# Turning u for the channel MLP: 96 TensorE transposes replaced by transposing DMAs of 16-bit halves

## The chip, the cores and the metric

The kernel runs on one core of a Trainium2 chip. The metric is the device time of one launch in microseconds (us); lower is better. The kernel before takes 856.54 us, the median of three runs from 856.44 to 856.61.

A core has five engines that run side by side, each with its own instruction stream in program order: TensorE (PE in the profile; PEld is its weight load), VectorE (DVE), ScalarE (ACT), GpSimd (POOL) and SyncE (SP). SyncE computes nothing here; it issues transfers, which 16 DMA engines carry out. Engines wait for one another on semaphores. An instruction that waits holds back all that stands behind it on its own engine.

## What is computed

A routed attention, then an MLP mixer. There are 4 batches of 768 positions with 8 heads of 64, so the attention gives `x` of 4 x 768 x 512 f32. The change lies in the second part:

```python
xt = x.transpose(0, 2, 1)
h = np.maximum(xt @ w_tok1, 0.0) @ w_tok2      # token MLP, over the 768 positions
u = x + h.transpose(0, 2, 1)
h2 = np.maximum(u @ w_ch1, 0.0) @ w_ch2        # channel MLP, 512 -> 1536 -> 512
return (u + h2).astype(np.float32)
```

TensorE contracts over the partition, the first of the two dimensions of on-chip memory. `u` is kept with positions on the partitions, and `u @ w_ch1` contracts over the 512 features, so `u` has to be turned: features on the partitions, positions along the row. How that turn is made is what the change is about.

## The kernel before, in words

**Stages.** The attention fills the first part of the time. From some 320 us on the token MLP runs, as a list of 32 steps named `ends`: `tok1(b, t)` and `tok2(b, j)`, the latter adding into `xs[b][:, j]`, so that the tile `xs[b]` (128 partitions x 6 x 512 f32) turns from `x` into `u` in place. Beside these steps weights are rounded and summed (`beside`). From 404 us on the channel MLP runs, batch by batch.

**The channel MLP.** Its two layers are each a 2x2 block product with seven products in place of eight, which needs sums of blocks of the weights (`left_weights`, `right_weights`) and of the turned `u` (`R` with T1 to T4). A batch has two parts of the 1536 hidden features. In each part come three first-layer chunks (`ch1_chunk`: hidden features from the turned `u`) and then three second-layer chunks (`ch2_chunk`: back to 512 features, added into `xs[b]`). `chunk` writes out the order of a chunk's products on TensorE: A11·B11, then the *deferred* last product of the chunk before (A22·T4, kept in `late`), then S1·T1, A12·B21, S2·T2, S4·B22, S3·T3. After each product `done` has VectorE or ScalarE empty the PSUM tile. In the first layer ScalarE has six instructions a chunk (L679, L683, L690, L703); in the second layer the chunks have none on ScalarE.

**The turned u.** The tile `uT` holds one batch: 2 halves of the positions (`n`) x 4 groups of 128 features (`f`) x 384 positions. There is one buffer, so a batch's `uT` can be filled only when the last first-layer chunk of the batch before has read it. `turn_u(b, n)` (L590) fills half `n`: for each `f` three TensorE transposes (L599) into a PSUM tile `pt`, then one copy to `uT` (L603), in turn on ScalarE and VectorE. With `n == 1` four subtractions on VectorE follow (T1 to T4, 128x768 f32 each). For batch 0 both calls stand between token steps (L896), when 11 and 9 steps are left. For batch b+1 they stand after the first and second of the three second-layer chunks of batch b's part 1 (L913).

**Outputs.** In part 1 each row `xs[b][:, j]` is stored by SyncE as soon as it is done (L735), 256 KB each.

**A way of turning that is there already.** The attention turns its results with the DMA engines: `values` copies PSUM into `avrows`, low and high 16-bit halves of each f32 apart (L454), `pair_turn` issues a transposing DMA from SyncE, which moves 16-bit elements (L459), and `pair_put` interleaves the halves again into `x` (L472).

The scheduling is manual: each engine's instructions stand in the order in which the program calls them.

Of the kernel before, what the change touches and what calls it, by code (L numbers as in the profile page):

```python
# [8 lines left out]
F32 = mybir.dt.float32  # L9
BF16 = mybir.dt.bfloat16  # L10
U32 = mybir.dt.uint32
U16 = mybir.dt.uint16
# [5 lines left out]
B, H, S, D = 4, 8, 768, 64  # L18
C = 16
P = 128  # L20
NJ = S // P
DM = H * D
NF = DM // P
# [4 lines left out]
HJ = NJ // 2  # L28
HS = HJ * P
# [19 lines left out]
def kernel(  # L49
# [29 lines left out]
    nc = tc.nc  # L79
# [30 lines left out]
    pools = {}  # L110


    ident = const.tile([P, P], F32, name="ident")
# [15 lines left out]
    xs = [xpool.tile([P, NJ, DM], F32, name=f"x{b}") for b in range(B)]  # L129
# [392 lines left out]
    def tok1(b, t):  # L522
        if t == 0:
            h1s[b] = tokpool.tile([P, NT, DM], F32, name="h1", bufs=2)
        pf = mtile([P, DM], "ph1")
        for j in range(NJ):
            nc.tensor.matmul(  # L527
                pf, lhsT=W["tok1"][:, j, t * P : (t + 1) * P], rhs=xs[b][:, j],
                start=(j == 0), stop=(j == NJ - 1),
            )  # L530
        relu(h1s[b][:, t], pf)
# [17 lines left out]
    def sub(dst, a, b):  # L549
        nc.vector.tensor_tensor(out=dst, in0=a, in1=b, op=ALU.subtract)  # L550

    def add(dst, a, b):
        nc.vector.tensor_tensor(out=dst, in0=a, in1=b, op=ALU.add)  # L553

    def left_weights():

        w = W["ch1"]
        half = DCH // 2
        A = {
            f"A{i + 1}{j + 1}": w[:, 2 * j : 2 * j + 2, half * i : half * i + half]  # L560
            for i in range(2)
            for j in range(2)
        }
        extra = pools["wsums"].tile([P, 3, 2, half], F32, name="w1s")
        A["S1"], A["S2"], A["S4"] = (extra[:, i] for i in range(3))
        yield lambda: add(A["S1"], A["A21"], A["A22"])
        yield lambda: sub(A["S2"], A["S1"], A["A11"])
        yield lambda: sub(A["A21"], A["A11"], A["A21"])
        yield lambda: sub(A["S4"], A["A12"], A["S2"])
        A["S3"] = A["A21"]  # L570
        pools["A"] = A
# [15 lines left out]
        B_["T3"] = B_["B12"]  # L587
        pools["B"] = B_

    def turn_u(b, n):  # L590

        if n == 0:
            pools["uT"] = pools["u"].tile([P, 2, NF, HS], F32, name="uT")
            pools["uTs"] = pools["u"].tile([P, 3, NF // 2, HS], F32, name="uTs")
        uT, uTs = pools["uT"], pools["uTs"]
        for f in range(NF):
            pt = pools["ps_m"].tile([P, HJ, P], F32, tag="YZ"[f % 2], name="pt")
            for i in range(HJ):
                nc.tensor.transpose(  # L599
                    out=pt[:, i], in_=xs[b][:, HJ * n + i, f * P : (f + 1) * P], identity=ident  # L600
                )
            copy = nc.vector.tensor_copy if f % 2 else nc.scalar.copy
            copy(out=uT[:, n, f], in_=pt.rearrange("p i t -> p (i t)"))  # L603
        if n == 1:
            R = {"B11": uT[:, 0, 0:2], "B21": uT[:, 0, 2:4], "B22": uT[:, 1, 2:4]}
            R["T1"], R["T2"], R["T4"] = (uTs[:, i] for i in range(3))
            R["T3"] = b12 = uT[:, 1, 0:2]
            sub(R["T1"], b12, R["B11"])
            sub(R["T2"], R["B22"], R["T1"])
            sub(R["T3"], R["B22"], b12)  # L610
            sub(R["T4"], R["B21"], R["T2"])
            pools["R"] = R

    late = []

    def chunk(n, product, done, last=False):

# [40 lines left out]
    def ch1_chunk(part, i):  # L658

        c = 3 * part + i  # L660
        if i == 0:
            pools["h2"] = {
                k: pools["mlp"].tile([P, 3, HS], F32, name="h" + k)
                for k in ("A11", "A12", "A22", "S1", "S2", "S3", "S4")
            }
        A, R, h2 = pools["A"], pools["R"], pools["h2"]
        kept = {}

        def product(psum, a, r, start):
            for k in range(2):  # L670
                nc.tensor.matmul(  # L671
                    psum, lhsT=A[a][:, k, c * P : (c + 1) * P], rhs=R[r][:, k],
                    start=start and k == 0, stop=k == 1, skip_group_check=not start,
                )

        def done(name, psum):
            if name in ("p1", "p5", "u2"):
                kept[name] = pools["mlp"].tile([P, HS], F32, name=name, bufs=2)
                nc.scalar.copy(out=kept[name], in_=psum)  # L679
            elif name == "c11":  # L680
                a = h2["A11"][:, i]
                add(a, psum, kept["p1"])
                nc.scalar.activation(out=a, in_=a, func=ACT.Relu)  # L683
            elif name == "c12":
                kept["c12"] = pools["mlp"].tile([P, HS], F32, name="c12", bufs=2)
                add(kept["c12"], psum, kept["u2"])
            elif name == "c22":
                a = h2["A22"][:, i]
                add(a, psum, kept["p5"])
                nc.scalar.activation(out=a, in_=a, func=ACT.Relu)  # L690

                nc.vector.scalar_tensor_tensor(
                    out=h2["S3"][:, i], in0=kept["c12"], scalar=0.0, in1=h2["A11"][:, i],
                    op0=ALU.max, op1=ALU.subtract,
                )
                nc.vector.scalar_tensor_tensor(
                    out=h2["S1"][:, i], in0=kept["c12"], scalar=0.0, in1=a,
                    op0=ALU.max, op1=ALU.add,
                )
                sub(h2["S2"][:, i], h2["S1"][:, i], h2["A11"][:, i])  # L700
            else:
                a = h2["A12"][:, i]
                nc.scalar.activation(out=a, in_=psum, func=ACT.Relu)  # L703
                sub(h2["S4"][:, i], a, h2["S2"][:, i])

        chunk(HS, product, done)

    def ch2_chunk(b, part, i):

        h2, Bw = pools["h2"], pools["B"]  # L710
        u = {
            f"c{r + 1}{c + 1}": xs[b][:, HJ * r + i, 256 * c : 256 * c + 256]
            for r in range(2)
            for c in range(2)
        }
        kept = {}
        takes = {"p1": "c11", "p5": "c22", "u2": "c12"}
        gives = {"c11": "p1", "c22": "p5", "c12": "u2"}

        def product(psum, a, w, start):  # L720
            for k in range(3):
                nc.tensor.matmul(  # L722
                    psum, lhsT=h2[a][:, k, i * P : (i + 1) * P], rhs=Bw[w][:, 3 * part + k],
                    start=start and k == 0, stop=k == 2, skip_group_check=not start,
                )

        def done(name, psum):
            if name in takes:
                kept[name] = pools["mlp"].tile([P, DM // 2], F32, name=name, bufs=2)
                add(kept[name], psum, u[takes[name]])  # L730
            else:
                add(u[name], psum, kept[gives[name]] if name in gives else u[name])
                if part == 1 and name in ("c12", "c21"):
                    j = i + HJ * (name == "c21")
                    nc.sync.dma_start(  # L735
                        out[b].rearrange("(p j) m -> p j m", p=P)[:, j], xs[b][:, j]
                    )

        chunk(DM // 2, product, done, b == B - 1 and part == 1 and i == 2)

    good = const.tile([P, 3], F32, name="good")
# [79 lines left out]
    ends = [lambda t=t: tok1(0, t) for t in range(NT)]  # L821
# [66 lines left out]
    pools["wsums"] = pool("wsums", 1, side="right")  # L888
    pools["u"] = pool("upool", 1, side="right")
    beside = weights + list(left_weights())  # L890
    while ends:
        for _ in range(-(-len(beside) // len(ends))):
            beside.pop(0)()
        ends.pop(0)()
        if len(ends) in (11, 9):
            turn_u(0, len(ends) == 9)  # L896
    staging.close()
    tokens.close()
    pools["mlp"] = pool("mlp", 1)
# [1 line left out]
    for b in range(B):  # L901
        for part in range(2):
            for i in range(3):
                ch1_chunk(part, i)
                for _ in range(2):
                    if beside:
                        beside.pop(0)()
            for i in range(3):
                if b == B - 1 and part == 1 and i == 2:
                    both = fits_load()  # L910
                ch2_chunk(b, part, i)
                if part == 1 and i < 2 and b + 1 < B:
                    turn_u(b + 1, i)  # L913
            if b == 0:
                (fits_count if part else fits)()
    late.pop()()


    def general():
# [209 lines left out]
```

## Time and profile before

| | |
|---|---|
| time, median of three | 856.54 us |
| span of the profiled execution | 854.8 us |
| mean granted TensorE clock | 0.998 |
| TensorE busy from 404 to 514 us | 110.00 us |
| VectorE, ScalarE busy in the same stretch | 53.07, 19.10 us |
| share of the DMA engines in the same stretch | 0.03 |
| TensorE transposes `pt` at L599 | 96 |
| `uT` copies on ScalarE, on VectorE | 16 of 479 ns, 16 of 558 ns |
| subtractions T1 to T4 | 16 of some 950 ns |
| transposing DMAs of the attention | 16 `avcols`, 15 `ohT` |
| output stores | 24, landing 2.0 us after issue (median) |

How to read the views: a row of the costliest groups gives line, engine, operation, output<-input and count, then busy time and mean duration of one, then the idle time of the engine just before and what ended most of it. A row of a tile gives minimum, median and maximum duration in ns and the times of the first and last start. A row of the timeline gives start, length, engine, line, and in brackets the idle time before it with what ended it. The chain of waits follows the work that ended last back to the start, step by step, to whatever released each step. A TensorE record is longer than the pitch of such records, because matmuls overlap; the chain's pieces are pitches.

### The profile page before, as it was taken

What the parts mean: (1) busy time and instruction counts of PE and PEld (TensorE: products, weight loads), DVE (VectorE), ACT (ScalarE), POOL (GpSimd) and SP (SyncE); (2) the same over time, 40 slices, a digit from 0 to 9 for tenths busy, and PEclk for the clock granted to TensorE, in tenths of its full rate; (3) what the DMA queues carried; (4) which work ended last, traced back from release to release, by engine and by line L of the source; (5) the groups of instructions that cost most, each with busy time, mean ns of one, the idle gap of its engine ahead of it and who ended that gap; (6) DMA issues with size and microseconds to landing.
All of it is one profiled execution on the core that took longest, in us unless ns stands there. A gap on an engine that the chain in (4) does not pass through costs nothing.

```text
span 854.8 us, 10898 instructions
## 1 busy us (share of the span) xinstructions
PE 844.1 (99%) x4198; PEld 516.4 (60%) x4198; DVE 509.8 (60%) x864; ACT 327.9 (38%) x522; POOL 45.6 (5%) x40
## 2 busy tenths in 40 slices
PE   9999999999999999999999999999999999999996
PEld 4444444444444444444587686776866858768675
DVE  6879888989889853985643453424444334443332
ACT  5677678787777663410201202102112031120210
POOL 1001010110101001410000000000000000000000
PEclk9999999999999999999999999999999999999999
DMA  8786576778774323400000010000100000100001
GB/s 150 154 160 131 112 152 138 151 145 146 143 142 96 56 54 107 151 22 0 0 1 1 1 49 25 1 0 1 38 37 1 1 0 25 50 0 1 1 25 54
DMA packets 158365, 53.92 MB, mean 63 GB/s; under 512 B 147168, under 2 KB 151264, under 8 KB 158304
## 3 DMA queue, kind: packets, MB, share of 16 engines
q1 hardware_dynamic: 156704, 52.74, 28.7%
q8 instruction: 35, 0.57, 0.3%
q10 hardware_dynamic: 1600, 0.39, 0.2%
q14 instruction: 26, 0.21, 0.1%
HBM read 34.64 MB, written 6.29 MB: 48 GB/s over the span
## 4 chain that ended last, share of the span: by engine, by line
PE 88%; DVE 8%; issue 1%; SPq 1%; DMA 1%; ACT 0%; DVEq 0%; POOL 0%; POOLq 0%
PE sc L422 16%; PE pX L722 15%; PE pX L671 15%; PE av L447 11%; PE pZ L722 7%; PE pZ L671 7%; PE ph L527 4%; PE pY L722 4%; PE pY L671 4%; PE pu L536 3%; DVE sum L437 2%; PE pt L599 1%; DVE wh L215 1%; DVE wT L220 1%; PE small L483 1%; DVE wh L210 1%
## 5 line engine op out<-in xcount | busy, mean ns | idle before, releaser
L429 ACT ACTIVATE ex<-sc 128x768 f32<-128x768 f32 x192 | 149.2, 812 | 27.7 <-PE sc L422 16.1
L422 PE MATMUL sc<-qkT 64*128 64x384 f32 x768 | 155.1, 482 | 0.0
L437 DVE TENSOR_TENSOR sum<-sum,ex 128x768 f32<-128x768 f32 x128 | 127.7, 997 | 27.4 <-ACT ex L429 15.2
L447 PE MATMUL av<-ex,va 128*64 128x384 f32 x768 | 127.4, 488 | 0.0
L447 PEld LDWEIGHTS av<-ex,va 128*64 128x64 f32 x768 | 53.7, 137 | 71.7 <-issue 67.9
L422 PEld LDWEIGHTS sc<-qkT 64*128 64x128 f32 x768 | 68.5, 187 | 36.3 <-issue 35.7
L679 ACT COPY p<-pX 128x384 f32<-128x384 f32 x24 | 11.4, 475 | 149.7 <-PE pX L671 149.7
L671 PE MATMUL pX<-uT,wc 128*128 128x384 f32 x192 | 67.4, 487 | 0.0
L422 PE MATMUL sc<-ohT 64*128 64x384 bf16 x384 | 63.3, 324 | 0.5 <-DVE ohT L394 0.2
L671 PEld LDWEIGHTS pX<-uT,wc 128*128 128x128 f32 x192 | 36.2, 190 | 24.7 <-issue 1.0
L454 ACT COPY avrows<-av 128x768 uint16<-128x768 uint16 x32 | 25.6, 798 | 47.1 <-PE av L447 47.1
L227 POOL TENSOR_TENSOR wc<-wT,wup 128x512 int32<-128x512 int32 x24 | 33.0, 1376 | 191.3 <-DVE wT L220 191.3
L527 PE MATMUL ph<-x,wt 128*128 128x512 f32 x96 | 41.9, 594 | 0.7 <-DVE x L539 0.7
L536 PE MATMUL pu<-h,wt 128*128 128x512 f32 x96 | 42.0, 592 | 0.0
L422 PEld LDWEIGHTS <-ohT 64*128 64x128 bf16 x384 | 20.1, 94 | 35.9 <-issue 11.1
L553 DVE TENSOR_TENSOR c<-pZ,u 128x384 f32<-128x384 f32 x24 | 13.4, 558 | 46.9 <-PE pZ L671 46.9
L553 DVE TENSOR_TENSOR hA<-pY,p 128x384 f32<-128x384 f32 x24 | 13.4, 557 | 40.4 <-PE pY L671 40.4
L690 ACT ACTIVATE hA<-hA 128x384 f32<-128x384 f32 x24 | 12.6, 523 | 63.4 <-DVE hA L553 63.4
L553 DVE TENSOR_TENSOR x<-pX,x 128x256 f32<-128x256 f32 x24 | 10.2, 423 | 42.6 <-PE pX L722 42.6
L722 PE MATMUL pX<-w2s,hS 128*128 128x256 f32 x144 | 35.2, 380 | 0.0
L722 PE MATMUL pX<-wc,hA 128*128 128x256 f32 x144 | 35.0, 379 | 0.0
L722 PE MATMUL pZ<-w2s,hS 128*128 128x256 f32 x144 | 35.0, 379 | 0.0
(123 smaller groups left out, 1221.8 us busy)
## 6 DMA issues: line engine op xcount, KB each, us to landing
raw<-in_moe_w_ch_dram SPq DMA_DIRECT2D x24, 512.0 KB, 4.2
va<-in_v_dram SPq DMA_DIRECT2D x16, 384.0 KB, 3.6
out_dram<-x SPq DMA_DIRECT2D x24, 256.0 KB, 2.0
qk<-in_k_dram SPq DMA_DIRECT2D x60, 96.0 KB, 3.8
qk<-in_q_dram SPq DMA_DIRECT2D x60, 96.0 KB, 3.5
raw<-in_moe_w_tok_dram SPq DMA_DIRECT2D x3, 512.0 KB, 4.2
raw<-in_moe_w_tok_dram SPq DMA_DIRECT2D x4, 384.0 KB, 3.9
ex<-in_q_dram ACTq DMA_DIRECT2D x4, 96.0 KB, 3.3
```

The source lines that it names most:

```text
L227: nc.gpsimd.tensor_tensor(out=dst.bitcast(I32), in0=T, in1=up, op=ALU.add)
L422: nc.tensor.matmul(sc[:, h, 0:HS], lhsT=src[rows, 1, j], rhs=src[rows, 0, js], start=start, stop=not start,)
L429: nc.scalar.activation(out=ex, in_=sc[:, :, 0:HS], func=ACT.Exp, scale=SM_SCALE)
L437: nc.vector.tensor_tensor(out=acc, in0=acc if j > 1 else st["ex", qh, 0], in1=st["ex", qh, j], op=ALU.add)
L447: nc.tensor.matmul(av[h * D : (h + 1) * D], lhsT=st["va"][:, h, j], rhs=ex[:, h], start=(j == 0), stop=(j == NJ - 1),)
L454: nc.scalar.copy(out=st["rows"][:, qh], in_=av.bitcast(U16).rearrange("p (t w) -> p w t", w=2))
L527: nc.tensor.matmul(pf, lhsT=W["tok1"][:, j, t * P : (t + 1) * P], rhs=xs[b][:, j], start=(j == 0), stop=(j == NJ - 1),)
L536: nc.tensor.matmul(pu, lhsT=W["tok2"][:, t, j], rhs=h1s[b][:, t], start=(t == 0), stop=(t == NT - 1))
L553: nc.vector.tensor_tensor(out=dst, in0=a, in1=b, op=ALU.add)
L671: nc.tensor.matmul(psum, lhsT=A[a][:, k, c * P : (c + 1) * P], rhs=R[r][:, k], start=start and k == 0, stop=k == 1, skip_group_check=not s ...
L690: nc.scalar.activation(out=a, in_=a, func=ACT.Relu)
L722: nc.tensor.matmul(psum, lhsT=h2[a][:, k, i * P : (i + 1) * P], rhs=Bw[w][:, 3 * part + k], start=start and k == 0, stop=k == 2, skip_grou ...
```

## The change

`turn_u` with its transposes, its PSUM tiles and its copies is gone. Half a batch's feature group (128 partitions x 384 f32) is now a *piece*; a batch has eight. `u_take` has ScalarE copy a piece into `rows`, low and high halves apart, and SyncE issue a transposing DMA from `rows` into `cols`. `u_put` has ScalarE interleave `cols` into `uT`. Both `rows` and `cols` have two buffers. The steps of a batch are: take 0; take 1; put 0 and take 2; put 1 and take 3; and so on to put 7. `u_sums` holds the four subtractions.

Where they are called: for batch 0 one step after each token step from the point at which 17 are left, and `u_sums` when all token steps are through. For batch b+1 take 0 and take 1 after the first and second first-layer chunk of batch b's part 1, all other steps after the first second-layer chunk of that part, and `u_sums` after its third. The output stores are collected in `outs` and issued after a chunk's turning steps, so that the transposes stand ahead of them on SyncE.

The aim is to take the turning of `u` off TensorE and give it to the DMA engines and ScalarE.

```diff
-    def turn_u(b, n):
-
-        if n == 0:
+    def u_take(b, i):
+
+        n, f = divmod(i, NF)
+        x = xs[b][:, HJ * n : HJ * n + HJ, f * P : (f + 1) * P].bitcast(U16)
+        rows = pools["u"].tile([P, 2, HJ, P], U16, name="urows", bufs=2)
+        nc.scalar.copy(out=rows, in_=x.rearrange("p j (c w) -> p w j c", w=2))
+        cols = pools["u"].tile([P, 2, HJ, P], U16, name="ucols", bufs=2)
+        nc.sync.dma_start_transpose(
+            out=cols.rearrange("p w j t -> p (w j) t"),
+            in_=rows.rearrange("p w j c -> p (w j c)"),
+        )
+        pools["ucols", i] = cols
+
+    def u_put(i):
+        n, f = divmod(i, NF)
+        if i == 0:
             pools["uT"] = pools["u"].tile([P, 2, NF, HS], F32, name="uT")
-            pools["uTs"] = pools["u"].tile([P, 3, NF // 2, HS], F32, name="uTs")
-        uT, uTs = pools["uT"], pools["uTs"]
-        for f in range(NF):
-            pt = pools["ps_m"].tile([P, HJ, P], F32, tag="YZ"[f % 2], name="pt")
-            for i in range(HJ):
-                nc.tensor.transpose(
-                    out=pt[:, i], in_=xs[b][:, HJ * n + i, f * P : (f + 1) * P], identity=ident
-                )
-            copy = nc.vector.tensor_copy if f % 2 else nc.scalar.copy
-            copy(out=uT[:, n, f], in_=pt.rearrange("p i t -> p (i t)"))
-        if n == 1:
...
+        out = pools["uT"][:, n, f].bitcast(U16).rearrange("p (t w) -> p w t", w=2)
+        nc.scalar.copy(out=out, in_=pools.pop(("ucols", i)).rearrange("p w j t -> p w (j t)"))
+
+    def u_steps(b):
+
+        N = 2 * NF
+        for i in range(2):
+            yield lambda i=i: u_take(b, i)
+        for i in range(N):
+            yield lambda i=i: (u_put(i), i + 2 < N and u_take(b, i + 2))
+
+    def u_sums():
...
-        if len(ends) in (11, 9):
-            turn_u(0, len(ends) == 9)
+        if len(ends) < 18 and turning:
+            turning.pop(0)()
+    u_sums()
...
                 ch1_chunk(part, i)
+                if part == 1 and b + 1 < B:
+                    if i == 0:
+                        turning = list(u_steps(b + 1))
+                    if i < 2:
+                        turning.pop(0)()
...
                 ch2_chunk(b, part, i)
-                if part == 1 and i < 2 and b + 1 < B:
-                    turn_u(b + 1, i)
+                if part == 1 and i == 0:
+
+                    while turning:
+                        turning.pop(0)()
+                while outs:
+                    outs.pop(0)()
+            if part == 1 and b + 1 < B:
+                u_sums()
```

More of the change, by code (lines that the diff above doesn't have):

```diff
@@ L588, in right_weights @@
         pools["B"] = B_
-    def turn_u(b, n):
-        if n == 0:
-            pools["uT"] = pools["u"].tile([P, 2, NF, HS], F32, name="uT")
-            pools["uTs"] = pools["u"].tile([P, 3, NF // 2, HS], F32, name="uTs")
-        uT, uTs = pools["uT"], pools["uTs"]
-        for f in range(NF):
-            pt = pools["ps_m"].tile([P, HJ, P], F32, tag="YZ"[f % 2], name="pt")
-            for i in range(HJ):
-                nc.tensor.transpose(
-                    out=pt[:, i], in_=xs[b][:, HJ * n + i, f * P : (f + 1) * P], identity=ident
-                )
-            copy = nc.vector.tensor_copy if f % 2 else nc.scalar.copy
-            copy(out=uT[:, n, f], in_=pt.rearrange("p i t -> p (i t)"))
-        if n == 1:
[L605 to L612, printed above, removed]
@@ L614 @@
-    late = []
+    def u_take(b, i):
[9 more added lines that the diff above has]
+        pools["ucols", i] = cols
@@ new lines, in u_sums @@
+    def u_sums():
+        uT = pools["uT"]
+        uTs = pools["uTs"] = pools["u"].tile([P, 3, NF // 2, HS], F32, name="uTs")
+        R = {"B11": uT[:, 0, 0:2], "B21": uT[:, 0, 2:4], "B22": uT[:, 1, 2:4]}
+        R["T1"], R["T2"], R["T4"] = (uTs[:, i] for i in range(3))
+        R["T3"] = b12 = uT[:, 1, 0:2]
+        sub(R["T1"], b12, R["B11"])
+        sub(R["T2"], R["B22"], R["T1"])
+        sub(R["T3"], R["B22"], b12)
+        sub(R["T4"], R["B21"], R["T2"])
+        pools["R"] = R
+    late, outs = [], []
@@ L734, in done @@
                     j = i + HJ * (name == "c21")
-                    nc.sync.dma_start(
-                        out[b].rearrange("(p j) m -> p j m", p=P)[:, j], xs[b][:, j]
+                    outs.append(
+                        lambda: nc.sync.dma_start(
+                            out[b].rearrange("(p j) m -> p j m", p=P)[:, j], xs[b][:, j]
+                        )
                     )
@@ L890 @@
     beside = weights + list(left_weights())
+    turning = list(u_steps(0))
     while ends:
@@ L916 @@
     late.pop()()
+    for issue in outs:
+        issue()
     def general():
```

## The prediction

> **What bounds the kernel now.** I read the busy shares first, then the chain of waits, then the tile `pt`, which the change takes away.
>
> ```profile
> PE 844.1 (99%) x4198; PEld 516.4 (60%) x4198; DVE 509.8 (60%) x864; ACT 327.9 (38%) x522; POOL 45.6 (5%) x40
> ...
> PE 88%; DVE 8%; issue 1%; SPq 1%; DMA 1%; ACT 0%; DVEq 0%; POOL 0%; POOLq 0%
> ```
>
> TensorE is never without work for long, and 88% of the chain that ended last lies on it. The busy time of stretches says the same of the stage concerned: from 404 to 514 us TensorE is busy 110.00 of 110.00 us, ScalarE 19.10. So a TensorE instruction taken out of this stage shortens the kernel by its pitch, unless a new wait takes its place. The tile `pt` gives the number and form:
>
> ```profile
> L599 PE MATMUL pt<-ident,x x96: 272/273/293, 382.7 to 728.2; 128*128 128x128 f32 x96
> L603 ACT COPY uT<-pt x16: 479/479/482, 383.2 to 728.2; 128x384 f32<-128x384 f32 x16
> L603 DVE COPY uT<-pt x16: 556/558/558, 383.6 to 728.5; 128x384 f32<-128x384 f32 x16
> ```
>
> The 272 ns of one record are not its price, since transposes overlap. The price is the piece in the chain in order of time (start, length, what):
>
> ```profile
> 493.99 1.31 PE pt L599 x12
> 495.30 2.59 PE pX L722 x12
> ...
> 504.37 1.31 PE pt L599 x12
> ```
>
> Twelve transposes, one call of `turn_u`, take 1.31 us, and the next product follows at once.
>
> **What the Trainium skill says.** "Perfetto Trace Analysis", section "Identifying the Most-Contended Engine", warns that matmul busy time is no measure of distance from the peak; hence the chain's lengths instead of 96 x 272 ns = 26 us, which would be 2.5 times too much. The same page, section "DMA Instruction — HWDGE (DVE, Sync)", says that the recorded window of such an instruction leaves the data movement out. The trace agrees: SyncE's records for `avcols` are 1.3 to 3.0 us, the landing comes 3.7 to 6.9 us after issue; I use landings. "VectorE: DVE Perf Modes", section "The three transpose paths", prices a 128x128 bf16 block at 1309 ns by DMA. Six blocks in a row would be 7.9 us, an estimate; but here an `avcols` of 128x1536 halves, twelve blocks, lands in as little as 3.7 us, so blocks overlap and the trace decides. "ScalarE: Activation LUTs", section "What ACT_TABLE_LOAD costs", gives 186 ns + 0.833 ns per element for an ACTIVATE without pointer operands: 506 ns at 384 elements, 479 in the trace.
>
> **Part 1, the transposes go.** Eight calls of `turn_u`. Six lie between second-layer chunks at 1.31 us. The two of batch 0 lie in the token stage: the first starts at 382.72 and the next product at 384.05, so 1.33 us, and the second is the same (387.49 to 388.82). 6 x 1.31 + 2 x 1.33 = 10.5 us. In the chunk that followed the second turn, one product took 1.36 instead of 1.29 us (at 510.86, 622.43, 733.69), because VectorE, busy with the turn's copies and subtractions, gave back a PSUM buffer late; that goes too: 3 x 0.07 = 0.2. **Removed: 10.7 us.** The copies out of PSUM (8 x 0.96 us ScalarE, 8 x 1.11 us VectorE) were beside TensorE and count nothing.
>
> **Part 2, ScalarE's new work.** Each batch has 8 pieces of 128x384 f32 = 128x768 16-bit halves: a take (gather halves into `rows`) and a put (interleave them into `uT`). The nearest rows have the same size and the same split:
>
> ```profile
> L472 ACT COPY x<-avcols 128x768 uint16<-128x768 uint16 x32 | 31.3, 1047 | 0.0
> L454 ACT COPY avrows<-av 128x768 uint16<-128x768 uint16 x32 | 25.6, 798 | 47.1 <-PE av L447 47.1
> ```
>
> A put is L472 with another name, 1.05 us. A take is L454 with SBUF as its source, which no row shows: between 0.80 and 1.05, I take 0.80. 8 x 1.85 = 14.8 us a batch, instead of 1.9, on an engine with this timeline around the second layer's first chunk:
>
> ```profile
> 485.56 0.52 ACT L690 ACTIVATE hA<-hA 128x384 f32<-128x384 f32 x1 [2.64 <-DVE hA L553]
> 487.55 0.49 ACT L703 ACTIVATE hA<-pX 128x384 f32<-128x384 f32 x1 [1.47 <-PE pX L671]
> ```
>
> After 488.05 ScalarE has nothing but the copies of `pt` until 516.50, when it copies the next batch's first `pX`. The first two takes sit in first-layer chunks, after L690; the idle 1.47 us before L703 holds 0.80, and 1.05 too. Cost: nothing.
>
> **Part 3, the round trip.** Two `rows` and two `cols` buffers, so two pieces are in flight, and piece i+2 is taken when piece i is put. The landing time is from
>
> ```profile
> avcols<-avrows SPq DMA_TRANSPOSE x16, 4.3
> ohT<-oh SPq DMA_TRANSPOSE x15, 3.8
> ```
>
> Both move twice the bytes of a piece, in a stage with DMA 50 to 80% busy; the two `avcols` after 295 us, with the queues nearly empty, land in 3.7. Bounds: 2.0 (a 256 KB store lands so in this stage) and 6.9 (the slowest `avcols`). I take 3.7. A round is put 1.05 + take 0.80 + landing 3.7 = 5.55 us. Pieces 0 and 1 landed long ago, so put 0 starts at 488.05, put 1 at 489.9, and put 7 three rounds after put 1, at 506.55; it ends at 507.6. Who waits for it? Behind the puts on ScalarE is the copy of the first `pX`, and VectorE's four subtractions. With 2.62 us of transposes gone, the end of the last chunk's last add moves from 515.26 (514.84 + 0.42 in the timeline) to 512.64, so the subtractions do not wait. TensorE itself needs the second of them, and `pX` copied, only at the product S2·T2, old 520.13, new 517.5. Put 7 has until 516.5: 8.9 us of slack, 3.0 a round, so landings up to 6.7 us cost nothing. The other two boundaries are the same code.
>
> SyncE: 8 transposes a batch, at most 1.43 us of issue each in a quiet stage, stand ahead of the outputs. Outputs then leave some 15 us later; nothing reuses those `x`, and the last batch has no transposes ahead of it. Cost: nothing.
>
> **Part 4, the subtractions move** behind the last add of the stage. Between batches T1 runs 512.64 to 513.6; TensorE has A11·B11 and the deferred A22·T4 first and wants T1 at 517.55 - 2.62 = 514.93. No wait. For batch 0 there is no deferred product:
>
> ```profile
> 404.27 1.45 PE L671 MATMUL pX<-uT,wc 128*128 128x384 f32 x4
> ...
> 404.47 0.69 DVE L539 TENSOR_TENSOR x<-pu,x 128x512 f32<-128x512 f32 x1 [1.02 <-PE pu L536]
> ...
> 405.56 0.81 PE L671 MATMUL pZ<-uTs,w1s 128*128 128x384 f32 x2
> ```
>
> T1 (0.95 us) can start when the add is nearly through, 0.60 us after its start by the pitch of such adds in a row: 405.07 to 406.02 against a `pZ` at 405.56. TensorE waits 0.5 to 0.9 us, I take 0.6, once. (Before, T1 was made at 389.5.) Batch 0's pieces are not late: ScalarE is idle from 366.4 to 381.2, five steps fit there, and by the round above put 7 ends near 394, with T1 due at 402.4.
>
> **Sum:** 856.54 - 10.7 + 0.6 = **846.4 us**.
>
> **Rivals.**
> - *The landing takes the place of the transposes.* If every piece lands in 6.9 us, a round is 8.75 us, put 7 ends at 489.9 + 26.25 + 1.05 = 517.2, 0.7 past its limit; three boundaries make 2 us: 848.4. For it: `avcols` had such landings. Against: then the DMA engines were loaded, here they are at 3 to 4% of their time.
> - *ScalarE's copies are slower than their rows and hold the first-layer chunk.* With 1.6 us takes (twice L454), the relu L703 starts 0.1 to 0.2 us late, six times, under VectorE's slack; a round grows by 0.8. About 846.4 to 847.5. Against: ScalarE prices go by elements here.
> - *Waits by whole tiles.* If a reader of `uT` waited for every earlier write of the tile, A11·B11 would wait for T3, written in place into `uT`. T3 ends 512.64 + 2 x 0.87 + 0.95 = 515.3, and A11·B11 is due at 514.86 - 2.62 = 512.2: 3.1 us, three times; for batch 0 402.5 + 2.7 = 405.2 against 401.6, 3.6. Together 12.9: 858.7, slower than before. Against: the store of one row of `x` at 493.18 lands 2.0 us later, yet VectorE writes another row of the same tile at 494.03, so waits go by region.
>
> **How the numbers follow.** Forecast 0.78 (845.6 to 847.3: takes and T1 wait at either end, landings 2.0 to 6.7), slow landing 0.10, slow ScalarE 0.05, whole tiles 0.05, something not seen 0.02. The range goes from 845.6, the sum with a shorter T1 wait and a 0.3 us gain at a boundary, to 848.8, the slow landing with the T1 wait at 0.9. The 0.2% bound is at 854.8 and 858.3: faster 0.92, within 0.03, slower 0.05 (whole tiles).
>
> **What would show it.** Part 1: no `pt` in the mixer stage, 96 TensorE instructions fewer, the chain going from one second-layer product to the next. Part 2: puts near 1.05 and takes near 0.80 us, ScalarE some 51 us busier in all (4 x 14.8 - 7.7). Part 3: 32 more transposes with landings under 4 us, last put of a batch near 20 us after its first, no TensorE wait on ScalarE. Part 4: one wait of `pZ` on VectorE at some 403 us and none at the other boundaries. Waits of TensorE on a put, on ScalarE's copy of `pX`, or on T3, adding to over 2 us, would make the prediction wrong.

## The result, and the profile after

The changed kernel takes **844.98 us** (median of four runs, 844.87 to 845.74) against 856.58 for the kernel before in the same comparison: ratio 0.9865, 95% interval 0.9848 to 0.9882, a gain of 11.6 us. The forecast was 846.4 with a range from 845.6: the direction and most of the size were right, the time lies 0.6 us below the range. So 1.4 us of gain came from a place that the prediction did not look at.

First the page of the kernel after, its busy shares and the shares of the chain of waits:

```profile
PE 833.0 (99%) x4102; PEld 506.3 (60%) x4102; DVE 501.5 (59%) x848; ACT 375.0 (44%) x570; POOL 45.7 (5%) x40
...
PE 92%; DVE 6%; issue 0%; ACT 0%; DMA 0%; DVEq 0%
```

There are 4198 - 4102 = 96 TensorE instructions fewer, ScalarE is 47 us busier, and TensorE still carries the chain. The chain in order of time where the first turn of batch 1 stood (start, length, what):

```profile
490.50 3.88 PE pX L740 x18
494.39 1.29 PE pZ L740 x6
```

Three products of 1.29 us follow one another where a turn of 1.31 us stood between them. The transposes' new home, in the tile `ucols` and the row of `urows` (durations minimum/median/maximum in ns):

```profile
L599 SPq DMA_TRANSPOSE ucols<-urows x32: 1209/1211/1565, 367.2 to 715.8; - x32
L610 ACT COPY uT<-ucols x32: 1037/1052/1059, 370.0 to 718.5; 128x768 uint16<-128x768 uint16 x32
...
DMA to landing us min/median/max: 2.7/2.8/3.9
```

```profile
L597 ACT COPY urows<-x x32: 814/818/829, 366.4 to 714.9; 128x768 uint16<-128x768 uint16 x32
```

A put is 1.05 us and a take 0.82, close to the 1.05 and 0.80 forecast; a landing is 2.8 us, better than the 3.7 taken. ScalarE's timeline at the first boundary between batches shows the round trip and its room:

```profile
485.36 0.49 ACT L721 ACTIVATE hA<-pX 128x384 f32<-128x384 f32 x1 [1.47 <-PE pX L689]
485.75 1.04 ACT L610 COPY uT<-ucols 128x768 uint16<-128x768 uint16 x1
...
490.29 1.05 ACT L610 COPY uT<-ucols 128x768 uint16<-128x768 uint16 x1 [1.17 <-DMA ucols<-urows]
...
502.34 1.06 ACT L610 COPY uT<-ucols 128x768 uint16<-128x768 uint16 x1 [0.75 <-DMA ucols<-urows]
511.57 0.48 ACT L697 COPY p<-pX 128x384 f32<-128x384 f32 x1 [8.18 <-PE pX L689]
```

A round, put 0 to put 2, takes 490.29 - 485.75 = 4.5 us. The last put ends at 503.4, and then ScalarE waits 8.2 us for TensorE, not TensorE for it. In the list of waits, TensorE has one wait in the new code, the one forecast, at the end of the token stage. The timeline shows 0.36 us of it; the run below that removes it puts its cost at 0.62:

```profile
402.26 0.95 DVE L550 TENSOR_TENSOR uTs<-uT 128x768 f32<-128x768 f32 x1
...
403.27 1.56 PE L689 MATMUL pZ<-uTs,w1s 128*128 128x384 f32 x4 [0.36 <-DVE uTs L550]
```

**Where the time went.** I cut the profiled executions at two events that both kernels have: the start of the first token product `ph`, and the start of the last VectorE add. Before, then after:

```profile
318.09 17.43 PE L527 MATMUL ph<-x,wt 128*128 128x512 f32 x40
...
847.54 0.42 DVE L553 TENSOR_TENSOR x<-pX,x 128x256 f32<-128x256 f32 x1 [0.87 <-PE pX L722]
```

```profile
317.93 17.43 PE L527 MATMUL ph<-x,wt 128*128 128x512 f32 x40
...
837.29 0.42 DVE L553 TENSOR_TENSOR x<-pX,x 128x256 f32<-128x256 f32 x1 [0.87 <-PE pX L740]
```

| | to first `ph` | first `ph` to last add | last add to end | span |
|---|---|---|---|---|
| before | 318.09 | 529.45 | 7.26 | 854.8 |
| after | 317.93 | 519.36 | 5.71 | 843.0 |
| difference | 0.16 | **10.09** | **1.55** | 11.8 |

Between the two events the gain is 10.09 us, and the prediction said 10.7 - 0.6 = 10.1. The first column differs between executions of any kernel here, from 317.87 to 318.82. What was missed is the last column: 1.55 us behind the start of the last add. There, rows of the source lines of the last branch (L1099, after it L1134) and of the end of the program (L1124, L1159) show SyncE's semaphore instructions. Before:

```profile
L1099 SPq EVENT_SEMAPHORE  x8: 17/17/17, 851.2 to 851.8; - x8
...
L1124 SPq EVENT_SEMAPHORE  x10: 17/28/28, 853.4 to 854.7; - x10
```

After:

```profile
L1134 SPq EVENT_SEMAPHORE  x8: 17/17/17, 841.1 to 841.6; - x8
...
L1159 SPq EVENT_SEMAPHORE  x10: 17/28/28, 841.7 to 842.9; - x10
```

Before, SyncE stands still from 851.8 to 853.4, with nothing in the list of waits to hold it; after, it goes on within 0.1 us. The DMA view from 0.4 us behind the start of the last add to the end of the span (6.8 us before, 5.3 us after) counts the transfers that bring instructions, 8 KB each on queue 14; before, then after:

```profile
q14 instruction: 5, 0.04, 1.9%
```

```profile
q14 instruction: 4, 0.03, 1.5%
```

In the kernel before, one of them starts at 851.78, beside the eighth semaphore instruction, and SyncE goes on 1.6 us later; the fifth starts at 854.04. In the kernel after, one starts at 841.77 too, and SyncE runs on beside it. So such a transfer does not stop SyncE by itself. Both traces fit if SyncE stands still only when it has come to the instructions that the transfer brings. This suggests theory A.

### The profile page after: what moved, and what is told of

It is laid out like the page before. It is cut to its first block, busy times and chain, and to the rows that moved or that the text cites. A ratio compares the mean times of both kernels' runs of the same rounds, so it can differ in the third digit from the quotient of the medians.

```text
span 843.0 us, 10784 instructions
## 1 busy us (share of the span) xinstructions
PE 833.0 (99%) x4102; PEld 506.3 (60%) x4102; DVE 501.5 (59%) x848; ACT 375.0 (44%) x570; POOL 45.7 (5%) x40
## 4 chain that ended last, share of the span: by engine, by line
PE 92%; DVE 6%; issue 0%; ACT 0%; DMA 0%; DVEq 0%
PE sc L422 18%; PE pX L740 15%; PE pX L689 15%; PE av L447 13%; PE pZ L689 7%; PE pZ L740 7%; PE ph L527 4%; PE pY L740 4%; PE pY L689 4%; PE pu L536 3%; PE small L483 1%; DVE wh L215 1%; PE small L302 1%; DVE wT L220 1%; DVE wh L210 1%; DVE sum L437 1%
## 5 line engine op out<-in xcount | busy, mean ns | idle before, releaser
L689 PEld LDWEIGHTS pX<-uT,wc 128*128 128x128 f32 x192 | 36.2, 190 | 24.7 <-issue 1.0
L610 ACT COPY uT<-ucols 128x768 uint16<-128x768 uint16 x32 | 33.7, 1052 | 19.7 <-DMA ucols<-urows 19.7
L689 PE MATMUL pZ<-uTs,w1s 128*128 128x384 f32 x96 | 35.0, 487 | 0.4 <-DVE uTs L550 0.4
```

The costliest lines, as they stand in the source:

```text
L610: nc.scalar.copy(out=out, in_=pools.pop(("ucols", i)).rearrange("p w j t -> p w (j t)"))
L689: nc.tensor.matmul(psum, lhsT=A[a][:, k, c * P : (c + 1) * P], rhs=R[r][:, k], start=start and k == 0, stop=k == 1, skip_group_check=not s ...
```

## Experiments

**Theory A**: the missing 1.4 us is a SyncE instruction fetch, which falls into the last microseconds or not depending on where the program's end lies in a fetched block. **Theory B**: the new order of the stores, or the transposes ahead of them, shortened the end. And for the main gain, **theory C**: it is TensorE's pitch and nothing else, and the round trip costs nothing as long as it meets a deadline; rivals are stated at each run.

### Never-executed instructions move the end

```diff
 # general(), the branch that is not taken
+        pad = gone.tile([P, 48, 8], F32, name="gpad")
+        for i in range(48):
+            nc.sync.dma_start(pad[:, i], v[0, 0, 0:P, 0:8])
```

> The kernel before, with 48 small loads added on SyncE in the general branch, which is never run: no executed instruction changes, but everything behind the branch on SyncE lies 48 instructions further on. Theory A (the part of the gain that the forecast lacks is a SyncE instruction fetch in the last microseconds, and whether one falls there depends on where the program's end lies in a fetched block of 8 KB): the gap of 1.61 us between SyncE's semaphore instructions at the end goes, the span behind the last VectorE add is 5.3 us instead of 6.8, the time is 855.0. Theory B (the stores' new order or the transposes ahead of them shortened the end): nothing changes, 856.5.

Measured: 855.25 us against 857.03, ratio 0.998 (0.9974 to 0.9987): 1.8 us faster by code that never runs. From the first `ph` to the last add it takes 529.49 us, as before; the end takes 5.6, or 5.2 from the end of the add, as the expectation counts. SyncE's rows of the branch and of the end, of this kernel:

```profile
L1103 SPq EVENT_SEMAPHORE  x8: 17/17/17, 852.0 to 852.6; - x8
...
L1128 SPq EVENT_SEMAPHORE  x10: 17/28/28, 852.6 to 853.9; - x10
```

The gap is gone.

The same with 80 loads in the changed kernel:

> The changed kernel, with 80 small loads added on SyncE in the branch that is never run. The change put 50 SyncE instructions into the stream by the trace's count, and 50 + 80 is 2 more than a block of 128 instructions[...]. Theory A: the end lies in its block as it did before the change, the gap of some 1.6 us comes back, and the time is 846.5, which is the forecast. Theory B: nothing changes, 845.0.

Measured: 846.97 us, ratio to the kernel before 0.9886 (0.9871 to 0.9901), against 0.9865 for the changed kernel. From first `ph` to last add 519.38, unchanged; the end takes 7.6. The gap is back, now inside the eight instructions of the branch, as the span of their starts shows:

```profile
L1138 SPq EVENT_SEMAPHORE  x8: 17/17/17, 841.0 to 843.4; - x8
```

And SyncE's list of waits has, beside the wait behind the branch that every kernel has (2.8 us), a second one of 1.9:

```profile
SPq L1138 <- SPq L1138: 4.7, 2, 2.8
```

With 128 loads in the kernel before:

> The kernel before with 128 small loads on SyncE in the branch that is never run[...]. Theory A (where the end lies in its fetched block of 128 instructions): the gap of 1.6 us is there as in the kernel before, 856.8. Rival (any added code in the branch removes the gap): 855.2, as with 48.

Measured: 857.04 against 856.91, ratio 1.0001 (0.9993 to 1.0009), the end takes 7.5 us. So it is not the presence of more code: 48 remove the gap, 128 leave it, here inside the eight instructions of the branch:

```profile
L1103 SPq EVENT_SEMAPHORE  x8: 17/17/17, 851.3 to 853.6; - x8
```

The place of the gap says more. In the kernel before it comes after the eighth of these instructions, with 128 loads after the seventh, and in the changed kernel with 80 loads after the fifth. These are one and three places earlier, and 128 + 1 = 129 and 50 + 80 + 1 = 131 are one and three more than 128. So a period of 128 instructions fits, if the added loads bring one instruction beyond their number; that one is not shown, since no trace records code that is not run. 8 KB is 128 of the 64-byte instructions that the Trainium skill ("Perfetto Trace Analysis", section "The 4-stage abstract model") states; no run here shows the size of an instruction. A shorter period of 64 would fit these runs too, one of 256 would not. The transfers agree: in all four profiles of this study that have the gap, five of 8 KB start behind the last add, and in the nine others four.

The first half of theory B was tried by itself, the new order of the stores with the transposes left on TensorE:

```diff
-                    nc.sync.dma_start(
-                        out[b].rearrange("(p j) m -> p j m", p=P)[:, j], xs[b][:, j]
-                    )
+                    outs.append(
+                        lambda: nc.sync.dma_start(
+                            out[b].rearrange("(p j) m -> p j m", p=P)[:, j], xs[b][:, j]
+                        )
+                    )
 ...
+                while outs:
+                    outs.pop(0)()
```

> The kernel before with the output stores collected and issued after each second-layer chunk, as in the change; the TensorE transposes stay. SyncE has as many instructions as before. Theory A: no change, 856.5, and the end keeps its gap. Theory B (the order of the stores is what shortens the end): some 855.0.

Measured: 857.04 against 857.03, ratio 1.0001 (0.9992 to 1.0009); the end takes 7.5 us, with the gap:

```profile
L1105 SPq EVENT_SEMAPHORE  x8: 17/17/17, 851.8 to 852.4; - x8
...
L1130 SPq EVENT_SEMAPHORE  x10: 17/28/28, 854.1 to 855.4; - x10
```

The other half, the transposes ahead of the stores, falls by the run with 80 loads, which has these transposes and has the gap. Theory A stands.

### The transposes put back, for nothing

```diff
+    def dead(b, n):
+        for f in range(NF):
+            pt = pools["ps_m"].tile([P, HJ, P], F32, tag="YZ"[f % 2], name="pt")
+            for i in range(HJ):
+                nc.tensor.transpose(
+                    out=pt[:, i], in_=xs[b][:, HJ * n + i, f * P : (f + 1) * P], identity=ident
+                )
 ...
+                if part == 1 and i < 2 and b + 1 < B:
+                    dead(b + 1, i)
```

> The changed kernel with the 96 TensorE transposes put back at their old places; their results are written to PSUM and read by nobody, so this part is work for nothing. Theory (the gain is TensorE's pitch and nothing else): 10.5 us over the changed kernel, less up to 0.6 where the first two give T1 no more room. Rival (part of the gain came from VectorE and ScalarE, which no longer copy pt): clearly less than 10.5.

Measured: 855.55 us against 845.29 for the changed kernel in the same comparison, 10.3 more. From first `ph` to last add: 529.84 against 519.36, 10.48. The chain has the old piece again:

```profile
495.11 1.31 PE pt L610 x12
```

So 10.5 us is TensorE's pitch alone. The copies that no longer run on VectorE and ScalarE gave nothing, apart from the 0.2 us at the boundaries, which did not come back: the product that took 1.36 us behind the second turn before takes 1.29 us here, too.

### The deadline of the round trip

One piece in flight instead of two:

```diff
-        rows = pools["u"].tile([P, 2, HJ, P], U16, name="urows", bufs=2)
+        rows = pools["u"].tile([P, 2, HJ, P], U16, name="urows", bufs=1)
-        cols = pools["u"].tile([P, 2, HJ, P], U16, name="ucols", bufs=2)
+        cols = pools["u"].tile([P, 2, HJ, P], U16, name="ucols", bufs=1)
```

> The changed kernel with one rows and one cols buffer, so that one piece is in flight at a time. Theory (a deadline): a piece takes put 1.05 + landing 2.8 + take 0.8 = 4.65 us, the last put of a batch ends at 485.75 + 7 x 4.65 + 1.05 = 519.4 instead of 503.4; T2 and the copy of pX then come at 520.3 for a product due at 515.4; three boundaries make 15 us: some 860. Rival (the turn is hidden whatever its length): 845.

Measured: 869.54 us, ratio to the kernel before 1.0138 (1.0121 to 1.0155): slower than the transposes it replaces, by more than expected. The last put of the first boundary ends at 520.6, 1.2 later than forecast, because one landing took 4.5 us. The waits of TensorE and, in stretches, its busy time with the granted clock (the number behind POOL's):

```profile
PE pX L689 <- DVE uTs L550: 16.1, 3, 5.7
```

```profile
521.00:525.00 4.00, 3.26 (x5) 1.85 (x6) 3.18 (x6) 1.10 (x3) 0.00 (x0) 0.50 0.52 194
525.00:530.00 5.00, 5.00 (x14) 2.83 (x13) 1.95 (x4) 0.67 (x2) 0.00 (x0) 0.80 0.06 21
530.00:535.00 5.00, 5.00 (x17) 2.94 (x16) 1.86 (x4) 1.93 (x5) 0.00 (x0) 1.00 0.01 3
```

The product S2·T2 starts at 521.74; in the changed kernel it starts at 515.41, and the first `ph` starts 0.25 us earlier there, so it is 6.1 us late. The wait is not its whole price: the granted clock is 0.50 after it (the 0.80 of the second stretch is a mean of 0.50 and 1.00), and the chain's next two pieces take 2.90 and 2.52 us instead of 1.29:

```profile
521.74 2.90 PE pX L689 x4
524.63 2.52 PE pZ L689 x4
```

The Trainium skill, "TensorE: Matmul & The Clock Gate", section "Why this matters for your kernels", warns of idle gaps over some 3 us between bursts of products; the trace agrees: in the idle gaps of 5.7, 4.7 and 5.7 us at the three boundaries the clock falls to 0.50, and it stays there for 6.8 us each time (520.2 to 527.0 at the first). Here 6.1 us of delay and 2.8 us more on the slow clock make 8.9 us at this boundary. From first `ph` to last add the kernel takes 24.7 us more (544.07 - 519.36).

Two buffers, but all further steps later in the batch:

```diff
-                if part == 1 and i == 0:
+                if part == 1 and i == 1:
 
                     while turning:
```

> The changed kernel with the turning steps of batch b+1 after the second second-layer chunk instead of the first. Theory (a deadline): the last put ends 7.8 us later, at 511.2, and the first product that needs it (S2.T2, by way of T2 and of the copy of pX) is due at 515.4, so nothing changes: 845.3. Rival (every us of the chain costs): some 20 us more.

Measured: 845.03 us, ratio 0.9862 (0.9847 to 0.9877), first `ph` to last add 519.34: nothing changes. The last put of the first boundary ends at 508.1, earlier than forecast: ScalarE makes the first two puts at 485.99 in any case, since nothing stands ahead of them there. What the place in the program delays is the third transpose on SyncE, which then stands behind a store that waits for its row of `x`.

With `i == 2`:

> The changed kernel with the turning steps after the third second-layer chunk. The last put ends at 518.9, T2 at 519.9 for a product due at 515.4: a wait of 4.5 us at three boundaries, 858.8, if a wait costs its length; with a lower granted TensorE clock after the wait, as the kernel with one buffer showed (2.7 to 2.9 us lost beside each wait), 867. Without a deadline: 845.3.

Measured: 853.95 us, ratio 0.9966 (0.9953 to 0.9979), first `ph` to last add 528.00, so 8.6 us more, and neither of the two sizes given. The deadline holds, but by the same early start of the first round the last put ends at 515.1 instead of 518.9. The chain of waits and the waits of TensorE:

```profile
500.17 0.33 SPq L754
...
500.60 2.75 DMA ucols<-urows
```

```profile
PE pX L689 <- DVE uTs L550: 4.4, 3, 1.8
PE pX L689 <- ACT u L697: 1.7, 3, 0.6
```

A store (L754) releases the transpose behind it on SyncE; that is what "ahead of the outputs" avoids. T2 ends at 516.1, TensorE waits 0.75 us in the record and starts S2·T2 at 516.28, and 0.6 more for a copy that ScalarE then makes late; the product after that starts at 522.39 instead of 520.65 with `i == 1`, where the first `ph` starts 0.14 us later, so 1.9 us are lost here. Such short waits left the clock at 1.00 in the stretches from 505 to 530 us, and the longer ones of 1.8 us at the other two boundaries left it there, too (from 620 to 640 and from 735 to 750 us).

### Batch 0's subtractions earlier

```diff
             turning.pop(0)()
-    u_sums()
+        if len(ends) == 5:
+            u_sums()
```

> The changed kernel with batch 0's four subtractions called when five token steps are left, instead of behind the last one. The last piece of batch 0 is put at 391.7 us and five steps are left at some 393, so the subtractions find their data. Theory: the one wait of TensorE on T1 (0.63 us) goes, 844.3 to 844.4. Rival (the subtractions hold back VectorE's token adds, so PSUM tiles come free late, 3.5 us of work against four tiles of 1.72 us): the wait is only moved, 845.0 or slower.

Measured: 844.54 us, ratio to the kernel before 0.9855 (0.984 to 0.987). Repeated beside the changed kernel itself:

> The changed kernel as it is, for a common reference on this chip: 11.6 us under the kernel before.

> The changed kernel with batch 0's subtractions at five steps left, now beside the changed kernel itself. Theory: 0.63 us under it. Rival: no difference.

Measured: 845.29 us (0.9865, 0.9849 to 0.9882) for the changed kernel and 844.46 us (0.9857, 0.984 to 0.9873) for this one. The intervals overlap, so the times alone do not settle 0.8 us. The trace does: from first `ph` to last add 518.74 and 518.73 in the two profiles, against 519.36 in both of the changed kernel, 0.62 us less. The chain of the changed kernel has two VectorE pieces there; that of the repeated run has none:

```profile
401.66 0.69 DVE x L539
402.35 0.87 DVE uTs L550
```

```profile
401.84 1.29 PE pX L689 x4
403.13 1.29 PE pZ L689 x4
```

The four subtractions now run ahead of the last token steps.

## Why the prediction was wrong, and where it was right

**The step that failed** is the last one, "Sum: 856.54 - 10.7 + 0.6". It takes off the terms of the changed stage and carries everything else over, and so assumes that the 7.26 us behind the last add stay 7.26. They became 5.71, and this is 1.55 of the gain. The change had put 32 transposes and 18 semaphore instructions into SyncE's stream; they cost nothing in time, but moved the program's end 50 instructions further on in this stream. The gap of 1.6 us at the end of the kernel before went by that shift alone: 48 instructions that are never run take it out of the kernel before, 80 bring it back into the changed one, at 846.97 us. The prediction's view of what could move ended with TensorE; it left 0.02 for something not seen, and that is what came. That the place of the code moves the end is shown by the runs; that SyncE waits there for a transfer of instructions is inferred from the gap, its place and the count of transfers, since no record names their receiver.

Point by point:

- *Part 1, 10.7 us.* Right: 10.48 for the transposes by the run that puts them back, and 0.2 at the boundaries.
- *Part 2, ScalarE's work costs nothing.* Right: put 1.05 and take 0.82 us, no wait of TensorE on ScalarE in the new code. ScalarE became 47 us busier, not 51: neighbouring puts and takes overlap by some 0.1 us, which a sum of durations counts twice and busy time once.
- *Part 3, the round trip costs nothing.* Right, with a landing of 2.8 us in place of 3.7; the last put ends at 503.4 and not 507.6. The deadline itself is shown by the two runs that miss it.
- *Part 4, one wait of 0.6 us on T1.* Right: 0.62 by the run that removes it, and none at the other boundaries. That the size came so close is in part luck: the two times worked out for it, 406.02 and 405.56, give 0.46, and 0.6 was picked from 0.5 to 0.9.
- *Rivals.* Slow landings did not occur in the changed kernel (3.9 us at most in the profile shown), slow copies neither (1.06 us at most for a put, 0.83 for a take). But the reason given against slow copies, that ScalarE's prices go by elements, does not hold as it stands: the prediction's own two rows have 768 elements each at 1047 and 798 ns. Waits by whole tiles would have held A11·B11 for T3; its products start on time.
- *The slow landing's price*, had it come, was too small in the prediction, which charged "0.7 past its limit" with 0.7 us. The run with the latest turning was 0.7 late at its first boundary (T2 at 516.1 for 515.4) and lost 1.9 us there, since the copies and adds queued behind were late too, and 8.6 in all; and a wait of several us also lowers the granted clock.

## What to carry to other kernels

When one engine is busy without gaps, the price of taking an instruction from it is its pitch in the chain, and the question left is a deadline: the work that went to other engines here was free as long as its last piece landed before the first product that needs it, and once it didn't, a long wait cost its length and then the slow clock behind it. Put transfers with a deadline ahead of those without on the issuing engine. When a gain of one or two us has to be understood, cut the trace at events that both kernels have and compare the start, the work and the end apart; an end that changes by over 1 us with nothing in it can be a matter of where instructions lie, and a few that are never executed test it.

## What the runs showed of the hardware

- Code that is never executed changed the time by 1.8 us: SyncE stood still for 1.6 to 1.9 us near the end, and whether and where it did so followed the number of instructions that lay ahead of it. That it waits there for a block of instructions is inferred.
- A transposing DMA of half the size (768 in place of 1536 halves per partition) landed in 2.8 us instead of the 3.7 of the two that found the queues nearly empty. As an estimate from these two figures, 0.9 us go with 768 halves and 1.9 us are fixed.
- In idle gaps of 4.7 to 5.7 us the granted TensorE clock fell to 0.50 and stayed there for 6.8 us, and the two next products at the first of them took 2.8 us more than their pitch; in waits of up to 1.8 us it stayed at 1.00.
